# H stage: the low part of each slot product subtracted by GpSimd instead of VectorE, with the order of the stage hung on VectorE's last step

## The chip, the cores and the metric

The kernel runs on one core of a Trainium2 chip. The metric is the device time of one execution in microseconds (us), the median of a few runs. The engines of the core are TensorE (PE in the profile; its weight loads are PEld), VectorE (DVE), ScalarE (ACT), GpSimd (POOL) and SyncE (SP, which here issues the transfers).

## The reference

Block-causal attention over 8 batches and 8 heads (576 positions, head size 64), then a soft mixture of experts (32 slots, 8 experts), then a bilinear layer:

```python
x = attention(q, k, v)                  # 4608 x 512
logits = x @ phi                        # 4608 x 32
slot_input = softmax(logits, 0).T @ x   # 32 x 512
slot_out = experts(slot_input)          # 32 x 512, relu(si @ w1[e]) @ w2[e]
y = softmax(logits, 1) @ slot_out       # 4608 x 512, c @ slot_out
out = (((y @ w1) * (y @ w2)) @ w3) @ w_out
```

## The kernel before

The kernel uses that y has only rank 32. With A = slot_out @ w1 and B = slot_out @ w2 (32 x 1024 each), `(y @ w1) * (y @ w2)` is a sum over pairs of slots of c_s c_t A_s B_t. So it builds H, one row for each pair of slots, as the products of slots (A_s B_t + B_s A_t) times W = w3 @ w_out, and the last stage multiplies the products c_s c_t of each token by H.

The stages follow one another: attention with the gathering of the slots, then the experts mixed with the making of W, then the **H stage**, then the **final stage**. The change lies in the H stage.

The matmuls run on operands in the type fp32r, which is coarser than fp32. Every operand is therefore split in a high and a low part: ScalarE's copy makes the high part, a subtraction makes the low part, and three matmuls (high by high, high by low, low by high) make one product.

The H stage goes over eight blocks f of 128 columns of the hidden size. For each, `slot_products(f)` issues on VectorE two multiplications of 128x512 (L1114 into G, L1115 into T), their sum (L1116, in place in G), and a halving of 32 columns (L1119). ScalarE then casts G to the high part Gh (L1121), and VectorE subtracts G - Gh to make the low part Gl (L1122). `h_chunk(k, f)` issues three matmuls for each k from 0 to 3 (L1135), which sum over f in PSUM: 12 for one f, 96 in all. The pairs of a slot with its opposite are made by GpSimd in L1125 to L1127 and multiplied in `h_last` (L1141). L1160 to L1169 finish that part; L1169 is a VectorE subtraction that reads one operand from PSUM.

`evacuate(k)` takes a finished part of H out of PSUM: ScalarE's cast to Hhi (L1144) and VectorE's subtraction to Hlo (L1145).

The final stage goes over 12 groups of 384 tokens. `products(u)` makes the products of slot weights: VectorE multiplies four times (L1210) and once more for the half group (L1216), ScalarE casts (L1211, L1217, L1218), and the low parts are subtracted by VectorE for k = 0 and 2 and by GpSimd for k = 1 and 3 (L1213), and by VectorE in L1219. Then come the matmuls with H (L1238, L1240) and the copy out (L1241).

A scheduler orders the instructions of each engine, here as it sees fit, from a model of the times. Two things bind it. `tc.issue_after(ins)` puts VectorE's instructions of a block behind `ins` in VectorE's queue. Block f of the slot products stands behind L1119 of block f - 1. And `self.fences` collects one instruction for each f (entries 0 to 7) and one for each `evacuate` (entries 8 to 11); the final stage's first group stands behind entry 7, its second and third behind entry 11. `G_st` and `Gr_st` have four places, so block f writes where block f - 4 has been read.

Of the kernel before, what the change touches and what calls it, by code (L numbers as in the profile page):

```python
# [7 lines left out]
F32 = mybir.dt.float32  # L8
# [3 lines left out]
ALU = mybir.AluOpType  # L12
# [804 lines left out]
class Rest:  # L817
# [81 lines left out]
    def run(self, out):  # L899
        nc, tc, io, keep = self.nc, self.tc, self.io, self.keep  # L900
        ident = keep["ident"]
        with ExitStack() as ctx:
# [182 lines left out]
            for dc in range(4):  # L1085
                for g in range(4):
                    w = self.wA if g < 2 else self.wB
                    f = 512 * (g % 2)
# [19 lines left out]
            def slot_products(f):  # L1108

                G, T = G_st[f % 4][:, 0:512], G_st[f % 4][:, 512:1024]  # L1110
                rot = lambda t: bass.AP(t.tensor, t[:, f, 0:1].offset, [list(t.ap[0]), [4, 4], [1, 32], [1, 4]])
                flat = lambda t: bass.AP(t.tensor, t[:, f, 0:1].offset, [list(t.ap[0]), [0, 4], [1, 32], [0, 4]])
                cols = lambda t: t.rearrange("p (k s i) -> p k s i", k=4, i=4)
                nc.vector.tensor_tensor(cols(G), flat(AT), rot(BT), op=ALU.mult)  # L1114
                nc.vector.tensor_tensor(cols(T), flat(BT), rot(AT), op=ALU.mult)  # L1115
                nc.vector.tensor_tensor(G, G, T, op=ALU.add)  # L1116

                own = cols(G)[:, 0, :, 0]
                add = nc.vector.tensor_scalar(own, own, 0.5, None, op0=ALU.mult).ins  # L1119
                Gh, Gl = (Gr_st[f % 4][:, 512 * i:512 * i + 512] for i in range(2))  # L1120
                nc.scalar.copy(Gh, G)  # L1121
                return Gh, Gl, nc.vector.tensor_tensor(Gl, G, Gh.bitcast(F32), op=ALU.subtract).ins, add  # L1122


            nc.gpsimd.tensor_tensor(G16[:, :, 0:16], AT[:, :, 0:16], BT[:, :, 16:32], op=ALU.mult)  # L1125
# [5 lines left out]
            def h_chunk(k, f):  # L1131
                Gh, Gl = terms[f]
                Wh, Wl = w_terms[f]
                for i, (a, b) in enumerate(((Gh, Wh), (Gh, Wl), (Gl, Wh))):
                    nc.tensor.matmul(Hp[k], lhsT=a[:, 128 * k:128 * k + 128], rhs=b,  # L1135
                                     start=f == 0 and i == 0, stop=f == 7 and i == 2)


            def h_last(f):
                g = f % 4  # L1140
                nc.tensor.matmul(Hp[4][32 * g:32 * g + 32], lhsT=G16[:, f], rhs=W[f], start=f < 4, stop=f >= 4)  # L1141
# [4 lines left out]

            for f in range(8):
                with tc.issue_after(gfence) if f else nullcontext():
                    Gh, Gl, last_op, add = slot_products(f)
                gfence = add  # L1150
                terms[f] = Gh, Gl
                self.fences.append(last_op)
                if f < 6:
                    for k in range(4):
                        h_chunk(k, f)
                    h_last(f)
# [192 lines left out]
```

## Time and profile before

| | |
|---|---|
| median of 3 runs | 575.46 us (574.84 to 575.87) |
| profiled execution | 577.33 us |
| its span, first to last instruction | 575.5 us |
| mean granted clock of TensorE | 0.979 of full |
| H stage, from the first slot product to the last matmul of L1135 | 431.3 to 458.9 us |

The span is that of the profiled execution, in which 1.8 us lie around the instructions; times in the trace are us from the start of the span. Timeline rows merge neighbouring instructions of one line: "x2" is two, and the duration is that of both. Number in brackets is the time that the engine was idle before, and behind the arrow what ended it.

### The profile page before, as it was taken

Reading aid. Unit: us, or ns where it says so; the run is one execution under the profiler, and the core shown is the slowest. Engines: PE = TensorE matmul, PEld = TensorE weight load, DVE = VectorE, ACT = ScalarE, POOL = GpSimd, SP = SyncE. Lnnn points to the kernel's source line nnn. Section 1 sums busy time; section 2 is a strip of 40 time slices with the busy share of each in tenths; the row PEclk is TensorE's granted clock in tenths of the full one; section 3 lists DMA queues with packets and bytes.
Section 4 is the critical chain, followed back from the end, with each engine's and each line's share of the span. In section 5 each row is a group of like instructions: output and inputs, shape, how many; then the busy total and the mean of one; then the engine's idle time right before and its main releaser. Section 6 shows DMA issues by size and latency. Waiting matters only on the chain.

```text
span 575.5 us, 13898 instructions
## 1 busy us (share of the span) xinstructions
PE 554.7 (96%) x5470; PEld 418.6 (73%) x5470; DVE 397.6 (69%) x701; ACT 321.4 (56%) x625; POOL 336.5 (58%) x246
## 2 busy tenths in 40 slices
PE   6999999999999999999999869999999999999997
PEld 3887778787887787878878545565656778888885
DVE  6678798888988979889832548652619987647550
ACT  4656668586686686876855235423433453535441
POOL 6887897978979979889776019212532122313220
PEclk9899999999999999999999978999999989999999
DMA  7255666566547365665276647999904047564732
GB/s 250 90 179 187 208 251 225 160 204 210 169 168 225 119 225 161 205 208 170 80 237 216 267 165 303 409 421 426 412 10 151 14 135 234 175 230 161 234 122 109
DMA packets 39193, 116.96 MB, mean 203 GB/s; under 512 B 5324, under 2 KB 15548, under 8 KB 37064
## 3 DMA queue, kind: packets, MB, share of 16 engines
q1 hardware_dynamic: 38948, 116.00, 58.0%
q8 instruction: 43, 0.70, 0.5%
q14 instruction: 22, 0.18, 0.1%
q10 hardware_dynamic: 180, 0.07, 0.0%
HBM read 105.75 MB, written 10.45 MB: 202 GB/s over the span
## 4 chain that ended last, share of the span: by engine, by line
PE 87%; DVE 8%; DMA 2%; ACT 2%; issue 1%; ACTq 0%; DVEq 0%
PE ps L400 19%; PE ps L1238 18%; PE ps L433 15%; PE ps L938 6%; PE ps L360 5%; PE ps L449 4%; PE ps L557 3%; PE ps L1048 3%; PE ps L1020 3%; PE ps L500 2%; PE ps L606 2%; PE ps L1240 1%; DVE bm L364 1%; DMA win<-in_moe_w 1%; DVE g_stage L1116 1%; PE ps L45 1%
## 5 line engine op out<-in xcount | busy, mean ns | idle before, releaser
L364 DVE TENSOR_REDUCE bm<-ps 128x10 f32<-128x640 f32 (+2 forms) x128 | 122.2, 987 | 33.5 <-PE ps L360 23.8
L400 PE MATMUL ps<-set 64*128 64x320 f32 (+4 forms) x1152 | 112.7, 304 | 0.5 <-ACT PTb L408 0.4
L400 PEld LDWEIGHTS ps<-set 64*128 64x128 f32 x1152 | 89.8, 186 | 5.5 <-issue 1.6
L1238 PE MATMUL ps<-H,Ph 128*128 128x512 f32 x288 | 91.5, 400 | 1.7 <-DVE H L1145 1.7
L348 POOL TENSOR_TENSOR set<-raw,set 128x1152 fp32r<-128x1152 f32 x32 | 84.9, 2657 | 8.2 <-ACT set L341 7.0
L1213 POOL TENSOR_TENSOR Pl<-rot,Ph 128x384 fp32r<-128x384 f32 x24 | 29.9, 1263 | 90.7 <-ACT Ph L1211 90.7
L418 POOL TENSOR_TENSOR acc<-PTa,PTb 128x640 f32<-128x640 f32 x32 | 49.9, 1558 | 35.8 <-ACT PTb L408 26.5
L1238 PEld LDWEIGHTS ps<-H,Ph 128*128 128x128 f32 x288 | 55.0, 191 | 15.6 <-DVE H L1145 2.1
L400 PE MATMUL ps<-shift 64*128 64x320 f32 (+4 forms) x384 | 58.5, 299 | 0.0
L1238 PE MATMUL ps<-H,Pl 128*128 128x512 f32 x144 | 57.4, 399 | 0.0
L1241 ACT COPY o<-ps 128x512 f32<-128x512 f32 x36 | 21.1, 587 | 57.3 <-PE ps L1240 56.8
L938 PE MATMUL ps<-wo,w 128*128 128x512 f32 x192 | 51.5, 409 | 0.0
L418 POOL TENSOR_TENSOR acc<-acc,PTc 128x640 f32<-128x640 f32 x31 | 48.3, 1556 | 2.0
L408 ACT ACTIVATE PTa<-ps 128x1024 f32<-128x1024 f32 x32 | 32.9, 1027 | 27.9 <-PE ps L400 22.9
L360 PE MATMUL ps<-set 64*128 64x320 f32 (+4 forms) x384 | 46.5, 317 | 0.3 <-ACT set L344 0.2
L938 PEld LDWEIGHTS ps<-wo,w 128*128 128x128 f32 x192 | 34.3, 190 | 16.8 <-issue 9.6
L442 ACT COPY xT<-ps 128x320 f32<-128x320 f32 (+1 forms) x64 | 25.5, 399 | 36.7 <-PE ps L437 28.2
L408 ACT ACTIVATE PTc<-ps 128x640 f32<-128x640 f32 (+1 forms) x64 | 39.8, 651 | 8.1 <-PE ps L400 8.1
L433 PE MATMUL ps<-PTc,v 128*64 128x320 f32 (+1 forms) x256 | 43.6, 419 | 0.0
L491 POOL TENSOR_TENSOR xT<-xT,shift 128x576 f32<-128x576 f32 x28 | 39.5, 1423 | 0.0
L1210 DVE TENSOR_TENSOR rot<-rot,crep 128x384 f32<-128x384 f32 x48 | 34.7, 755 | 5.9 <-DMA rot<-cs 5.2
L341 ACT CAST set<-raw 128x1152 fp32r<-128x1152 f32 x31 | 35.6, 1150 | 3.6 <-DMA raw<-in_qk 3.6
(234 smaller groups left out, 1115.3 us busy)
## 6 DMA issues: line engine op xcount, KB each, us to landing
win<-in_moe_w SPq DMA_DIRECT2D x16, 2048.0 KB
raw<-in_qk SPq DMA_DIRECT2D x32, 576.0 KB
v<-in_v SPq DMA_DIRECT2D x32, 320.0 KB
rot<-cs SPq DMA_DIRECT2D x48, 192.0 KB
out<-o SPq DMA_DIRECT2D x11, 768.0 KB
raw<-in_moe_w SPq DMA_DIRECT2D x16, 512.0 KB
shift<-rr SPq DMA_DIRECT2D x56, 144.0 KB
w3raw<-in_w3T SPq DMA_DIRECT2D x14, 512.0 KB
```

Of the source, the lines that this page charges most:

```text
L341: self.nc.scalar.copy(hi, self.raw[n])
L348: self.nc.gpsimd.tensor_tensor(lo, self.raw.pop(n), hi.bitcast(F32), op=ALU.subtract)
L360: self.nc.tensor.matmul(ps[:, h, o:o + kn], lhsT=qh[r, q0:q0 + 128], rhs=kh[r, k0:k0 + kn], start=True, stop=True)
L364: self.nc.vector.tensor_reduce(self.bmb[n % 2][:, :, o:o + m // 64], self.st.pop(("M", n, i))[:, :, 0:m].rearrange("p h (n k) -> p h n k", ...
L400: self.nc.tensor.matmul(ps[:, h, o0:o0 + w], lhsT=lt[r, k] if i < 3 else lt[r], rhs=rt[r, q0:q0 + w], start=i == 0, stop=i == 3)
L408: self.nc.scalar.activation(out=out, in_=ps[:, :, 0:sum(g[3] for g in self.UNITS[u])], func=AF.Exp, scale=SCALE)
L418: eng.tensor_tensor(acc[:, :, lo:hi], a, b, op=ALU.add)
L433: mm(ps[64 * h:64 * h + 64, q0 - lo:q1 - lo], lhsT=v[:, 128 * j + 64 * h:128 * j + 64 * h + 64], rhs=pt[:, h, o:o + q1 - q0], start=j == 0 ...
L491: self.nc.gpsimd.tensor_tensor(x, x, self.rb[:, i], op=ALU.mult)
L938: nc.tensor.matmul(p, lhsT=a[:, o], rhs=b, start=c + i == 0, stop=c == 7 and i == 2)
L1210: nc.vector.tensor_tensor(p, p, crep, op=ALU.mult)
L1238: nc.tensor.matmul(ps, lhsT=a[:, k, r], rhs=b[:, k], start=n == 0, stop=False)
```

## The change

The subtraction that makes Gl is issued on GpSimd instead of VectorE. `slot_products` returns the halving L1119 (`add`), which as before is what the next block's VectorE instructions stand behind. It is now also what goes into `self.fences`: entry 7, behind which the final stage's first group stands on VectorE, was L1122 of block 7 and is now L1119 of block 7.

```diff
                 Gh, Gl = (Gr_st[f % 4][:, 512 * i:512 * i + 512] for i in range(2))
                 nc.scalar.copy(Gh, G)
-                return Gh, Gl, nc.vector.tensor_tensor(Gl, G, Gh.bitcast(F32), op=ALU.subtract).ins, add
+                nc.gpsimd.tensor_tensor(Gl, G, Gh.bitcast(F32), op=ALU.subtract)
+                return Gh, Gl, add
...
                 with tc.issue_after(gfence) if f else nullcontext():
-                    Gh, Gl, last_op, add = slot_products(f)
-                gfence = add
+                    Gh, Gl, gfence = slot_products(f)
                 terms[f] = Gh, Gl
-                self.fences.append(last_op)
+                self.fences.append(gfence)
```

## Rows read from the trace of the kernel before

**Rows 1.** The page: busy time by engine, and the chain that ended last.

```profile
PE 554.7 (96%) x5470; PEld 418.6 (73%) x5470; DVE 397.6 (69%) x701; ACT 321.4 (56%) x625; POOL 336.5 (58%) x246
...
PE 87%; DVE 8%; DMA 2%; ACT 2%; issue 1%; ACTq 0%; DVEq 0%
```

**Rows 2.** The chain in order of time (start, us, what), 425 to 475.

```profile
434.09 0.59 DVE g_stage L1114
434.68 0.60 DVE g_stage L1115
435.28 0.60 DVE g_stage L1122
435.89 1.71 DVE g_stage L1116
...
455.80 1.96 DVE rot L1210 x4
...
460.82 0.70 DVE H L1145
...
461.57 8.57 PE ps L1238 x29
```

**Rows 3.** The waits, 425 to 475: us in total, times, longest.

```profile
PE ps L1238 <- DVE H L1145: 1.7, 1, 1.7
...
DVE g_stage L1122 <- ACT g_stage L1121: 0.8, 1, 0.8
```

**Rows 4.** Busy time by stretch: PE, PEld, DVE, ACT, POOL, TensorE's granted clock, DMA.

```profile
458.90:462.30 3.40, 1.71 (x7) 1.13 (x7) 3.37 (x6) 2.82 (x6) 1.03 (x1) 1.00 0.24 64
462.30:465.70 3.40, 3.40 (x9) 2.66 (x9) 3.34 (x7) 1.19 (x3) 0.14 (x1) 0.50 0.83 253
465.70:469.10 3.40, 3.40 (x16) 2.74 (x16) 3.40 (x5) 1.75 (x4) 2.35 (x2) 1.00 0.18 59
```

**Rows 5.** The timeline of TensorE: the matmuls of blocks 4 to 7.

```profile
447.88 11.04 PE L1135 MATMUL ps<-W,g_stage 128*128 128x512 f32 x48
```

**Rows 6.** The timeline of VectorE: L1169, one turn, and the last block.

```profile
441.67 0.69 DVE L1169 TENSOR_TENSOR H<-ps,H 32x512 fp32r<-32x512 f32 x1
442.39 0.69 DVE L1122 TENSOR_TENSOR g_stage<-g_stage,g_stage 128x512 fp32r<-128x512 f32 x1
...
446.45 0.69 DVE L1114 TENSOR_TENSOR g_stage<-AB,AB 128x512 f32<-128x512 f32 x1
447.05 0.69 DVE L1115 TENSOR_TENSOR g_stage<-AB,AB 128x512 f32<-128x512 f32 x1
447.65 0.69 DVE L1122 TENSOR_TENSOR g_stage<-g_stage,g_stage 128x512 fp32r<-128x512 f32 x1
448.26 0.68 DVE L1116 TENSOR_TENSOR g_stage<-g_stage 128x512 f32<-128x512 f32 x1
448.97 0.20 DVE L1119 TENSOR_SCALAR g_stage<-g_stage 128x32 f32<-128x32 f32 x1
449.08 0.68 DVE L1114 TENSOR_TENSOR g_stage<-AB,AB 128x512 f32<-128x512 f32 x1
...
454.23 0.20 DVE L1119 TENSOR_SCALAR g_stage<-g_stage 128x32 f32<-128x32 f32 x1
455.19 0.69 DVE L1122 TENSOR_TENSOR g_stage<-g_stage,g_stage 128x512 fp32r<-128x512 f32 x1 [0.76 <-ACT g_stage L1121]
```

**Rows 7.** The timeline of GpSimd: subtractions without VectorE beside them, then with it.

```profile
423.28 2.52 POOL L1074 TENSOR_TENSOR g_stage<-wO,g_stage 128x512 fp32r<-128x512 f32 x2 [0.75 <-ACT g_stage L1073]
...
435.34 1.70 POOL L897 TENSOR_TENSOR W<-wO,W 128x512 fp32r<-128x512 f32 x1 [1.30 <-ACT W L896]
457.45 1.19 POOL L1213 TENSOR_TENSOR Pl<-rot,Ph 128x384 fp32r<-128x384 f32 x1 [20.41 <-ACT Ph L1211]
```

**Rows 8.** The timeline of VectorE in the same places.

```profile
435.20 0.68 DVE L1122 TENSOR_TENSOR g_stage<-g_stage,g_stage 128x512 fp32r<-128x512 f32 x1
435.81 1.78 DVE L1116 TENSOR_TENSOR g_stage<-g_stage 128x512 f32<-128x512 f32 x1
...
457.67 1.38 DVE L1216 TENSOR_TENSOR half<-half 32x384 f32<-32x384 f32 x1
```

**Rows 9.** The line L1216: ns min/median/max, first and last start.

```profile
L1216 DVE TENSOR_TENSOR half<-half x12: 539/546/1376, 457.7 to 544.7; 32x384 f32<-32x384 f32 x12
```

**Rows 10.** The timeline of all engines: VectorE with a PSUM operand beside GpSimd.

```profile
413.98 1.30 POOL L897 TENSOR_TENSOR w<-f,w 128x512 fp32r<-128x512 f32 x1 [0.73 <-ACT w L896]
414.01 0.69 DVE L842 SCALAR_TENSOR_TENSOR ps<-w3raw,ps 128x512 int32<-128x512 int32 x1
```

**Rows 11.** The timeline of ScalarE: the last cast of a slot product, the first evacuation.

```profile
454.54 0.62 ACT L1121 CAST g_stage<-g_stage 128x512 fp32r<-128x512 f32 x1 [2.01 <-DVE g_stage L1119]
...
458.27 0.59 ACT L1144 CAST H<-ps 128x512 fp32r<-128x512 f32 x1 [0.44 <-PE ps L1135]
```

## Prediction

> **What bounds the kernel now.** I read the page first: TensorE is busy for 96% of the span and carries 87% of the chain that ended last, VectorE 8% [rows 1]. A change to VectorE matters only where it is on that chain, so I read the chain in order of time next. From 434.09 to 461.5 us it is VectorE's queue without a break: the slot products of blocks 1 to 7, then the first group's products, then L1145 at 460.82, which releases the final stage's matmuls at 461.57 [rows 2]. From there TensorE carries it to the end. So the end of the kernel hangs on when VectorE reaches the first L1145, and a microsecond there is a microsecond of the total.
>
> The waits say the same from TensorE's side: one wait of 1.7 us for L1145 [rows 3]. [...]
>
> During the H stage itself TensorE isn't waiting: the 48 matmuls of blocks 4 to 7 take 11.04 us, 0.23 each and 2.72 for one block's twelve [rows 5]. VectorE's turn is 449.08 - 446.45 = 2.63 us a block [rows 6], so it stays just ahead. TensorE's queue isn't in the order of the source: in that order the first matmuls of block 7 would come at about 454.0 (447.88 + 27 x 0.227), but the cast that feeds them ends at 455.16 [rows 11] and the 48 have no gap. And the first evacuation starts only at 458.27 [rows 11], some nine matmuls into block 7, if block 7 starts at 447.88 + 36 x 0.227 = 456.04. So a block's eight matmuls on the high part go first and the four on the low part last. The low part has room of about 1.8 us; the high part has 456.04 - 455.16 = 0.9 us.
>
> **The change part by part.** All terms are changes of the start of the first L1145 in VectorE's queue, counted from L1119 of block 0, ahead of which the change puts nothing.
>
> Removed: the L1122 that stand between L1115 and L1116. Each takes 448.26 - 447.65 = 0.61 us of the queue [rows 6]; seven of them are 4.27 us. The last L1122 goes with its wait of 0.76 us for ScalarE: L1210 starts at 455.80 [rows 2], and could start 0.10 us after the start of L1119 at 454.23, as L1114 does behind L1119 (449.08 - 448.97 = 0.11) [rows 6]. That the fence is now L1119 allows it. This takes 455.80 - 454.33 = 1.47 us. Together -5.74 us.
>
> Added: eight subtractions of 128x512 on GpSimd. Alone such a one takes 2.52 / 2 = 1.26 us, up to 1.30 [rows 7, 10], twice VectorE's time; that by itself would hide in the 1.8 us of room and in GpSimd's idle time, since it did nothing between 437.04 and 457.45 [rows 7]. But it doesn't run beside VectorE. The one L897 that fell into the slot products, 435.34 to 437.04, took 1.70 us, and L1116 beside it 1.78 instead of 0.68 [rows 7, 8]. The ends tell how: VectorE's L1122 ended at 435.88, GpSimd at 437.04, 1.16 later, L1116 at 437.59, another 0.55 later. They took turns, each waiting for the other's whole work. The final stage repeats it with 384 columns: L1216, 0.55 us at the median, took 1.38 beside L1213 [rows 8, 9]. So each subtraction moved to GpSimd costs VectorE's queue 1.78 - 0.68 = 1.10 us, at a place where it is never idle. Eight are 8.80 us: seven among the slot products, and the eighth among the first group's products, which also stand before L1145. Bounds: the 384-column row gives 1.38 - 0.55 = 0.83 each, 6.64 in all; the time of a subtraction alone, 1.26 to 1.30, some 10.2. I take 1.10, since it is the row of this shape, in this stage, on the same line L1116 that will stand behind it.
>
> [...] If the hold were the full 1.28 us, the sum would be +3.8 us; the row shows 1.10, as part of the GpSimd instruction passes under VectorE's, and +2.3.
>
> Covered: VectorE's instruction with one operand in PSUM, L1169, takes 442.39 - 441.67 = 0.72 us of the queue now [rows 6]. Instructions of that kind ran beside GpSimd unstretched: L842 in 0.69 us under an L897 of 1.30 [rows 10]. In the queue L1169 stands between L1115 and the place of L1122, just where GpSimd's turn will come, so the work hides in one of the holds: -0.72 us. If the scheduler puts it elsewhere, that is 0.
>
> [...]
>
> Nothing else costs. GpSimd's queue has L897 of W's last block ahead of or behind the first Gl; it isn't needed until block 7, and its hold of VectorE is paid before and after alike. Behind the last Gl wait two L1213 of the first group, whose holds are also paid in both. ScalarE's casts and the transfers by SP stay as they are; SP's loads for later groups wait for L1210 and move with it.
>
> Sum: 8.80 - 5.74 - 0.72 = **+2.34 us** at the first L1145. The turn grows from 2.63 to 2.63 - 0.61 + 1.10 = 3.12 us, above TensorE's 2.72, so TensorE begins to wait 0.4 us a block once the 0.9 us of room is used up, about block 4. Its last block then starts 7 x 0.49 - 0.72 - 0.9 = 1.8 us later, and L1145, 2.3 later, is still what it waits for last. The clock's fall I leave as it is, once, behind a wait that is somewhat longer. Against the profiled execution's own 577.33 us this makes 579.67; the median of the runs is 1.87 us below it, so 575.46 + 2.34 = **577.8 us**.
>
> **The rivals.** First, faster: GpSimd fits into gaps and VectorE really loses its eight instructions. The price that decides is that of a hold: 8h = 6.46, so below h = 0.81 us the first L1145 comes earlier, and for 0.2% (1.15 us) it must be under 0.66. [...] For it: VectorE's queue would be 5.7 us shorter. Against it: the stretched rows [rows 8, 9].
>
> Second, the clock stays at 1.00. TensorE's idle time is spread over blocks 4 to 7 as waits of 0.4 us, and the long wait falls elsewhere. [...] Against it: the wait at the end isn't shorter than the one that now precedes the fall.
>
> Third, worse: TensorE's waits make the clock fall once more, or the scheduler, which believes the low parts come as GpSimd's time says, orders TensorE's or ScalarE's queue so that a late operand blocks more behind it. [...]
>
> **How the numbers follow.** The likeliest case has 0.62, with its own range from 576.9 (holds of 0.99 us) to 578.5 (L1169 not covered). The faster rival has 0.09, as both overlaps in the rows are stretched; the second 0.15, the third 0.14. About 0.2% (1.15 us) is what a measurement of this kernel can tell from no change. Holds as in the 384-column row, 6.64 - 5.74 - 0.72 = +0.18, would also be no change, 575.6 us; this I count with a little of the likeliest case, so the same has 0.18, slower 0.73, faster 0.09. The range, 575.6 to 579.6, runs from these short holds to the second fall of the clock, and takes in holds as long as a subtraction alone (10.2 - 6.46 = 3.7 us, 579.2).
>
> **What would show it.** GpSimd's new subtractions should last about 1.5 us (waiting for their turn), L1116 behind them 1.7 to 1.8, and VectorE's turn about 3.1 us. The last L1119 should come near 457, the first L1145 near 463.2, and TensorE should restart near 463.9. L1135 should show waits of 0.3 to 0.5 us from block 4 on for the casts. The prediction is wrong if L1116 stays at 0.68 us beside GpSimd, if the turn stays under 2.7 us, or if L1145 stops being what the final stage waits for.

## The result and the profile after

The changed kernel took 579.79 us (median of 6 runs, 578.45 to 580.83) against 576.14 us (6 runs, 574.84 to 576.83) for the kernel before: a ratio of 1.0066, with a 95% interval of 1.0048 to 1.0085. Run again later (e8 below), it took 579.31 us against 576.60, a ratio of 1.0043 (1.0028 to 1.0057) with 23 runs of the kernel before. By these medians the change makes the kernel slower by 2.7 to 3.7 us.

In the changed file the lines from L1123 on have moved by one: the matmuls of the H stage are L1136, the evacuations L1145 (ScalarE) and L1146 (VectorE), `h_last` is L1142 and GpSimd's products L1126 to L1128. From L1147 to the end the numbers are as before. L1122 is now GpSimd's subtraction.

The page of the kernel after, busy time by engine and the chain that ended last:

```profile
PE 555.8 (96%) x5470; PEld 417.5 (72%) x5470; DVE 400.0 (69%) x693; ACT 321.4 (56%) x625; POOL 348.3 (60%) x254
...
PE 85%; DVE 9%; ACT 3%; DMA 2%; issue 1%; ACTq 0%; DVEq 0%
```

Against [rows 1], eight instructions have left VectorE and yet it is busy for 2.4 us more. GpSimd has eight more and 11.8 us. An instruction that waits for its turn counts as busy, as the rows of L1116 below show (1.67 us instead of 0.68).

The chain of the kernel after in order of time (start, us, what):

```profile
434.79 0.59 DVE g_stage L1114
...
457.53 3.91 DVE rot L1210 x4
461.44 0.46 DVE half L1216
461.90 1.75 DVE Pl L1213 x2
...
463.68 0.55 DVE Ph L1219
...
464.26 0.70 DVE H L1146
...
465.01 8.36 PE ps L1238 x28
```

This answers to [rows 2]. It is still VectorE's queue that leads to TensorE's restart, at 465.01 instead of 461.57. The first halving, ahead of which nothing was changed, came 0.71 us later (434.46 against 433.75). Between the last products of the first group and the first evacuation there now stands L1219, which wasn't there.

The timeline of VectorE after: the block beside L897, L1169, and one turn.

```profile
437.71 1.17 DVE L1119 TENSOR_SCALAR g_stage<-g_stage 128x32 f32<-128x32 f32 x1
...
443.22 0.69 DVE L1169 TENSOR_TENSOR H<-ps,H 32x512 fp32r<-32x512 f32 x1
443.94 0.94 DVE L1116 TENSOR_TENSOR g_stage<-g_stage 128x512 f32<-128x512 f32 x1
...
451.27 0.68 DVE L1114 TENSOR_TENSOR g_stage<-AB,AB 128x512 f32<-128x512 f32 x1
451.88 0.68 DVE L1115 TENSOR_TENSOR g_stage<-AB,AB 128x512 f32<-128x512 f32 x1
452.60 1.67 DVE L1116 TENSOR_TENSOR g_stage<-g_stage 128x512 f32<-128x512 f32 x1
454.30 0.20 DVE L1119 TENSOR_SCALAR g_stage<-g_stage 128x32 f32<-128x32 f32 x1
454.40 0.69 DVE L1114 TENSOR_TENSOR g_stage<-AB,AB 128x512 f32<-128x512 f32 x1
```

And of GpSimd:

```profile
437.09 1.74 POOL L897 TENSOR_TENSOR W<-wO,W 128x512 fp32r<-128x512 f32 x1
...
452.18 1.54 POOL L1122 TENSOR_TENSOR g_stage<-g_stage,g_stage 128x512 fp32r<-128x512 f32 x1 [1.58 <-ACT g_stage L1121]
455.30 1.54 POOL L1122 TENSOR_TENSOR g_stage<-g_stage,g_stage 128x512 fp32r<-128x512 f32 x1 [1.59 <-ACT g_stage L1121]
458.43 1.30 POOL L1122 TENSOR_TENSOR g_stage<-g_stage,g_stage 128x512 fp32r<-128x512 f32 x1 [1.59 <-ACT g_stage L1121]
```

The turn is 454.40 - 451.27 = 3.13 us, where [rows 6] give 2.63. L1116 lasts 1.67 us: L1122 runs from 452.18 to 453.72, and L1116 ends at 454.27, 0.55 later, as in [rows 7, 8]. Beside L1169 the same L1116 needs only 0.94, since part of GpSimd's turn has passed under L1169.

TensorE after, the matmuls of blocks 4 to 7 (timeline), and what TensorE waited for (us in total, times, longest):

```profile
449.00 12.42 PE L1136 MATMUL ps<-W,g_stage 128*128 128x512 f32 x48 [0.17 <-ACT g_stage L1121]
```

```profile
PEld ps L1136 <- ACT g_stage L1121: 2.4, 5, 0.6
PE ps L1238 <- ACT H L1145: 2.2, 1, 2.2
...
PE ps L1238 <- DVE H L1146: 0.4, 1, 0.4
```

The 48 matmuls take 12.42 us instead of 11.04 [rows 5]; in the stage as a whole, weight loads waited five times for the casts; and the wait ahead of the final stage is 2.2 + 0.4 us instead of 1.7 [rows 3]. No wait of TensorE for GpSimd's L1122 shows in this stage.

Most of that last wait is for ScalarE. Three of its four evacuations stood ahead of L1217 and L1218 before (the first at 458.27 [rows 11]); now all four stand behind them, in ScalarE's timeline:

```profile
461.94 0.51 ACT L1217 CAST Ph<-half 32x384 fp32r<-32x384 f32 x1
462.47 0.51 ACT L1218 CAST Ph<-half 32x384 fp32r<-32x384 f32 x1
463.00 2.05 ACT L1145 CAST H<-ps 128x512 fp32r<-128x512 f32 x4
```

TensorE started on the final stage behind the first of these casts, at 463.64, and stopped once more for L1146. L1146 still ends the wait, but by little: without L1219 it would have started at about 463.68, when that cast had just ended.

Busy time by stretch after, in the columns of [rows 4]:

```profile
465.07:468.48 3.41, 3.41 (x8) 2.73 (x9) 3.41 (x7) 1.23 (x3) 0.18 (x1) 0.50 0.82 226
468.48:471.89 3.41, 3.41 (x16) 2.71 (x15) 3.41 (x5) 1.71 (x4) 2.31 (x2) 1.00 0.29 91
```

The granted clock falls once behind the wait, to 0.50 for 3.4 us as before, and 8 matmuls start in that stretch where the next holds 16. By the 9 and 16 of [rows 4] I estimate the price of such a stretch at 7/16 x 3.4 = 1.5 us.

### The profile page after: what moved, and what is told of

It reads as the page before. It is cut to its first block, busy times and chain, and to the rows that moved or that the text cites. A ratio compares the mean times of both kernels' runs of the same rounds, so it can differ in the third digit from the quotient of the medians.

```text
span 579.0 us, 13898 instructions
## 1 busy us (share of the span) xinstructions
PE 555.8 (96%) x5470; PEld 417.5 (72%) x5470; DVE 400.0 (69%) x693; ACT 321.4 (56%) x625; POOL 348.3 (60%) x254
## 4 chain that ended last, share of the span: by engine, by line
PE 85%; DVE 9%; ACT 3%; DMA 2%; issue 1%; ACTq 0%; DVEq 0%
PE ps L400 19%; PE ps L1238 18%; PE ps L433 15%; PE ps L938 6%; PE ps L360 5%; PE ps L449 4%; PE ps L557 3%; PE ps L1048 3%; DVE g_stage L1116 2%; PE ps L1020 2%; PE ps L500 2%; PE ps L606 2%; PE ps L1240 1%; DVE bm L364 1%; DMA win<-in_moe_w 1%
## 5 line engine op out<-in xcount | busy, mean ns | idle before, releaser
L400 PE MATMUL ps<-set 64*128 64x320 f32 (+4 forms) x1152 | 112.4, 303 | 0.5 <-ACT PTb L408 0.4
L1210 DVE TENSOR_TENSOR rot<-rot,crep 128x384 f32<-128x384 f32 x48 | 36.3, 797 | 5.7 <-DMA rot<-cs 5.3
```

The costliest lines, as they stand in the source:

```text
L400: self.nc.tensor.matmul(ps[:, h, o0:o0 + w], lhsT=lt[r, k] if i < 3 else lt[r], rhs=rt[r, q0:q0 + w], start=i == 0, stop=i == 3)
L1210: nc.vector.tensor_tensor(p, p, crep, op=ALU.mult)
```

## The experiments

Theory A is the prediction's: GpSimd's subtraction and a VectorE instruction with two operands in SBUF take turns, as L897 and L1116 did before (1.70 us, and 1.78 instead of 0.68 [rows 7, 8]), so each subtraction moved costs VectorE's queue about 1.1 us, at a place where the final stage waits for that queue. Theory B: what costs is that GpSimd is slow, so that the low parts reach TensorE late. Theory C: the new fence, and the order that the scheduler makes of it, carry the loss.

Three numbers from each profile tell where a kernel's time lies. The **head** is the start of block 0's halving (L1119; L1120 in e6, e7, e9 and e10), ahead of which the kernels don't differ, other than those with operands in PSUM (e6, e7, e9, e10). The **lead** is from there to the start of VectorE's first evacuation. The **tail** is from TensorE's restart behind that evacuation to the end of the span. For the kernel before: head 433.75, lead 460.82 - 433.75 = 27.07, tail 575.54 - 461.57 = 113.97. Its first halving, in VectorE's timeline:

```profile
433.75 0.33 DVE L1119 TENSOR_SCALAR g_stage<-g_stage 128x32 f32<-128x32 f32 x1
```

| kernel | head | lead | tail | ratio to before (95%) |
|---|---|---|---|---|
| before | 433.75 | 27.07 | 113.97 | |
| after | 434.46 | 29.80 | 114.03 | 1.0066 (1.0048 to 1.0085) |
| e1 fence alone | 434.20 | 26.79 | 112.48 | 0.9972 (0.9959 to 0.9985) |
| e2 extra subtractions | 434.74 | 34.98 | 115.13 | 1.0161 (1.0139 to 1.0184) |
| e3 extra fills | 434.86 | 27.13 | 114.01 | 1.0008 (0.9989 to 1.0028) |
| e4 half of them moved | 434.77 | 27.80 | 112.41 | 0.9988 (0.9976 to 0.9999) |
| e5 L1219 later | 432.69 | 29.21 | 112.41 | 1.0033 (1.0019 to 1.0047) |
| e6 B and T in PSUM | 436.19 | 24.55 | 112.36 | 0.9949 (0.9930 to 0.9967) |
| e7 the same, VectorE subtracts | 434.17 | 25.98 | 112.42 | 0.9971 (0.9955 to 0.9987) |
| e8 after, again | 433.65 | 29.79 | 113.98 | 1.0043 (1.0028 to 1.0057) |
| e9 A and T in PSUM | 434.36 | 24.67 | 112.57 | 0.9954 (0.9936 to 0.9972) |
| e10 the same, VectorE subtracts | 433.37 | 26.13 | 112.42 | 0.9980 (0.9963 to 0.9997) |
| e11 e5, profiled again | 433.07 | 29.22 | 114.01 | |
| e12 before, profiled again | 435.12 | 27.06 | 114.00 | |

The lead repeats within 0.02 us (before and e12, after and e8, e5 and e11). The head differs by up to 1.4 us between profiles of one kernel. The tail is near one of two values: 114.0, when the clock fell behind the wait, and 112.4 to 112.6, when it didn't. Only e2, where the clock stayed down twice as long, has 115.1.

**e1: the fence alone**, subtraction on VectorE.

```diff
-                self.fences.append(last_op)
+                self.fences.append(add)
```

> The subtraction stays on VectorE; only the fence entries are L1119 instead of L1122. Theory A (GpSimd's subtraction and VectorE's two-operand instructions take turns, some 1.1 us a piece): the turn stays at 2.63 us; VectorE's wait of 0.76 us before the last L1122 is filled, but L1219 now stands ahead of the first evacuation (0.58 us), so the first evacuation moves by about -0.2 us and the time by -0.2 +- 0.5 us. Theory C (the fence and the order that the scheduler makes of it carry the loss): +2 us or more.

Measured: lead 26.79, 0.28 us shorter, as theory A has it; all turns as before. The time fell by 0.28% (1.6 us; the medians, 575.65 and 576.86, are 1.2 us apart), more than expected. In its profile TensorE's wait ahead of the final stage was 0.9 us instead of 1.7, as another 0.5 now lay inside the H stage (from the first matmul's start in L1135 to the last one's 23.1 us, 22.6 before), and the clock didn't fall (tail 112.48). Theory C, that fence and order carry the loss, falls. VectorE's timeline at the end shows what the fence does to the order:

```profile
454.79 1.96 DVE L1210 TENSOR_TENSOR rot<-rot,crep 128x384 f32<-128x384 f32 x4
456.66 1.37 DVE L1216 TENSOR_TENSOR half<-half 32x384 f32<-32x384 f32 x1
457.96 0.67 DVE L1122 TENSOR_TENSOR g_stage<-g_stage,g_stage 128x512 fp32r<-128x512 f32 x1
458.56 1.82 DVE L1213 TENSOR_TENSOR Pl<-rot,Ph 128x384 fp32r<-128x384 f32 x2
460.42 0.55 DVE L1219 TENSOR_TENSOR Ph<-half,Ph 32x384 fp32r<-32x384 f32 x1
461.00 2.48 DVE L1145 TENSOR_TENSOR H<-ps,H 128x512 fp32r<-128x512 f32 x4
```

L1219 stands ahead of the evacuation here too: it is the fence, not GpSimd, that brings it there. ScalarE's evacuations stand behind L1217 and L1218 here as well.

**e2: eight more subtractions on GpSimd that nobody waits for**, in the kernel before.

```diff
+                nc.gpsimd.tensor_tensor(T, G, Gh.bitcast(F32), op=ALU.subtract)
                 return Gh, Gl, nc.vector.tensor_tensor(Gl, G, Gh.bitcast(F32), op=ALU.subtract).ins, add
```

> The kernel before, with eight more subtractions of the same form on GpSimd, whose results (written into T, which is done with) nobody reads. Theory A: eight holds of 1.1 us less 0.72 of L1169 that is hidden in one: VectorE's turn 3.7 us, L1116 at 1.7 us, the time +7 to +8 us. Theory B (what costs is that GpSimd's own slowness makes the low parts late for TensorE): 0, since nothing waits for the extra results.

Measured: lead 34.98, 7.9 us longer; turns of 3.73; the time 1.6% (9.3 us) longer, more than the 7 to 8 expected. In the timelines of VectorE (L1123 is the subtraction here) and of GpSimd the two meet at another instruction:

```profile
447.85 0.68 DVE L1115 TENSOR_TENSOR g_stage<-AB,AB 128x512 f32<-128x512 f32 x1
448.45 1.78 DVE L1123 TENSOR_TENSOR g_stage<-g_stage,g_stage 128x512 fp32r<-128x512 f32 x1
450.16 0.68 DVE L1116 TENSOR_TENSOR g_stage<-g_stage 128x512 f32<-128x512 f32 x1
```

```profile
448.08 1.61 POOL L1122 TENSOR_TENSOR g_stage<-g_stage,g_stage 128x512 f32<-128x512 f32 x1 [2.11 <-ACT g_stage L1121]
```

The tail is 1.1 us longer as well: ahead of the final stage TensorE waited 1.2 us for ScalarE's evacuation and then 2.2 us for VectorE's, and the clock was down for 6.8 us. Nothing waits for these results, and VectorE loses 1.78 - 0.68 = 1.10 us a piece. Theory B, that a slow engine's late results cost the time, falls: GpSimd's presence costs it.

**e3: eight fills on GpSimd**, in the kernel before.

```diff
+                nc.gpsimd.memset(T, 0.0)
                 return Gh, Gl, nc.vector.tensor_tensor(Gl, G, Gh.bitcast(F32), op=ALU.subtract).ins, add
```

> The kernel before, with eight fills of T (128x512) on GpSimd: it writes but reads nothing. [...] Theory B: 0.

Measured: lead 27.13, turns 2.63, ratio 1.0008: nothing. A fill of 0.58 us lay beside L1114 without stretching it, in the timelines of VectorE and of GpSimd:

```profile
447.51 0.20 DVE L1119 TENSOR_SCALAR g_stage<-g_stage 128x32 f32<-128x32 f32 x1
447.61 0.68 DVE L1114 TENSOR_TENSOR g_stage<-AB,AB 128x512 f32<-128x512 f32 x1
```

```profile
447.60 0.58 POOL L1122 MEMSET g_stage<- 128x512 f32 x1 [2.17 <-DVE g_stage L1116]
```

Only the halving beside a fill was stretched, in four of the eight blocks: from 0.20 to 0.60 us in three and from 0.33 to 0.80 in the first, and the turns stayed as they were within 0.06 us. Had fills of 0.52 to 0.58 us held VectorE for their length, eight would have cost about 4.4 us, an estimate from these lengths; the lead grew by 0.06. So the fills, which only write, didn't hold the two-operand instructions (0.68 us beside one); the subtraction, which reads, did (1.78 us in e2).

**e4: half of the subtractions moved**, in the changed kernel.

```diff
-                nc.gpsimd.tensor_tensor(Gl, G, Gh.bitcast(F32), op=ALU.subtract)
+                (nc.vector if f % 2 else nc.gpsimd).tensor_tensor(Gl, G, Gh.bitcast(F32), op=ALU.subtract)
```

> The changed kernel with the odd blocks' subtraction back on VectorE. Theory A: four holds (4.4 us) for four L1122 (2.4 us), less 0.72 (L1169 hidden) and 0.76 (the wait gone), plus 0.58 (L1219 ahead): +1.1 us against the kernel before, turns of 3.1 us behind even blocks and 2.6 behind odd ones. Theory B: half of the measured loss, +1.8 us, with all turns alike. Theory C: the full loss, +3.6 us.

Measured: lead 27.80, 0.73 us longer than before (1.1 expected). The turns alternate, 3.12 behind an even block and 2.63 behind an odd one, which only theory A has. The time didn't rise, though: 0.9988. The profile shows a wait of 0.9 us ahead of the final stage and a clock that stayed up, 1.6 us less tail. The expectation left that out. How often the clock stayed up in the other runs isn't known.

**e5: L1219 behind the first evacuation**, in the changed kernel.

```diff
-                nc.vector.tensor_tensor(Ph[32:64, 4], p, Ph[0:32, 4].bitcast(F32), op=ALU.subtract)
+                with tc.issue_after(self.fences[8]) if u == 0 else nullcontext():
+                    nc.vector.tensor_tensor(Ph[32:64, 4], p, Ph[0:32, 4].bitcast(F32), op=ALU.subtract)
```

> The changed kernel, with the first group's L1219 put behind the first evacuation on VectorE. If its place ahead of the evacuation is the term that the prediction left out, the first evacuation comes 0.58 us earlier after the last L1119 than in the changed kernel, and the time is about 0.5 us less than with the change; if TensorE has other things to wait for, 0.

Measured: lead 29.21, 0.59 us shorter than with the change. In the lead, then, the place of L1219 is worth what its row says. The time, 578.65 us against 579.31 for the changed kernel beside it (e8), fits with 0.66 less but doesn't show it, since the two intervals overlap.

**e6: the change, but with B and T in PSUM**, so that L1114 to L1116 (here L1115 to L1117) read one operand each from SBUF. B is also kept in SBUF, where GpSimd's products read it as before: four more copies on ScalarE.

```diff
+            Bp, Tp = keep["ps"][:, 2].rearrange("p (f s) -> p f s", f=8), keep["ps"][:, 0]
-            for m, dst in ((0, AT), (1, BT)):
+            for m, dst in ((0, AT), (1, Bp), (1, BT)):
...
-                G, T = G_st[f % 4][:, 0:512], G_st[f % 4][:, 512:1024]
+                G, T = G_st[f % 4][:, 0:512], Tp
...
-                nc.vector.tensor_tensor(cols(G), flat(AT), rot(BT), op=ALU.mult)
-                nc.vector.tensor_tensor(cols(T), flat(BT), rot(AT), op=ALU.mult)
+                nc.vector.tensor_tensor(cols(G), flat(AT), rot(Bp), op=ALU.mult)
+                nc.vector.tensor_tensor(cols(T), flat(Bp), rot(AT), op=ALU.mult)
```

> The changed kernel, with B also copied into PSUM and T kept in PSUM, so that L1114 to L1116 read only one operand each from SBUF. Theory A: VectorE and GpSimd run side by side: turn 2.0 to 2.1 us, no stretched L1116, GpSimd's subtraction 1.3 us; TensorE's matmuls then set the stage's pace at 2.72 us a block, and the wait of 1.7 us ahead of the final stage shrinks below 0.5 us: 572.5 to 574.5 us, faster than both kernels, less up to 0.8 us for the four more copies on ScalarE. Theory B: the low parts are as late as with the change, +3 us or more against the kernel before.

Measured: 573.79 us, ratio 0.9949, faster than both kernels, although the head holds a wait of 1.2 us of VectorE for the copy into PSUM. VectorE's and GpSimd's timelines:

```profile
448.99 0.69 DVE L1116 TENSOR_TENSOR ps<-ps,AB 128x512 f32<-128x512 f32 x1
449.71 0.69 DVE L1117 TENSOR_TENSOR g_stage<-g_stage,ps 128x512 f32<-128x512 f32 x1
```

```profile
449.29 1.30 POOL L1123 TENSOR_TENSOR g_stage<-g_stage,g_stage 128x512 fp32r<-128x512 f32 x1 [0.88 <-ACT g_stage L1122]
```

The same two instructions now lie over each other at the durations that they have alone, 0.69 and 1.30 us. The turn is 2.15 us, TensorE sets the stage's pace again, and its timeline shows no wait from the stage's 48 matmuls into the final stage:

```profile
449.95 11.04 PE L1137 MATMUL ps<-W,g_stage 128*128 128x512 f32 x48
460.83 1.16 PE L1239 MATMUL ps<-H,Ph 128*128 128x512 f32 x4
```

This is the direct test of theory A: with one operand of each of these three VectorE instructions out of SBUF, and the subtraction still on GpSimd, the loss turns into a gain of some 2.8 us. How much of it the operands in PSUM give by themselves is e7's question.

**e7: the same operands in PSUM, the subtraction on VectorE** (the edit of e6 in the kernel before).

> The kernel before (subtraction on VectorE) with the same operands in PSUM: what the PSUM copy does by itself. Theory A: only the one hold by L897 goes: the first evacuation 1.1 us earlier, turn still 2.63 us, the time -1.1 us, less up to 0.4 for the copies. Theory B: 0 to +0.5 us.

Measured: lead 25.98, 1.09 us shorter, turns of 2.62: the one hold by L897 is gone. The time is 0.29% (1.7 us) less, with the clock up in its profile. Of e6's gain, then, PSUM alone gives more than half (576.60 - 574.97 = 1.6 us), and moving the subtraction the rest (574.97 - 573.79 = 1.2 us).

**e8: the changed kernel once more.**

> The changed kernel itself once more. The two profiles put +2.73 us into the H stage and +0.71 us into what runs before it, where the instructions are the same. If that 0.71 us is chance, more runs give +2.7 +- 0.5 us; if it belongs to the change, +3.5 us or more, and the start of the slot products is again late by 0.7 us.

Measured: 579.31 us, 1.0043, medians 2.7 us apart; head 433.65, so not late this time; lead 29.79. The 0.71 us ahead of the stage was chance.

**e9: A instead of B in PSUM**, copied there by VectorE; ScalarE copies B, and A into SBUF for GpSimd.

```diff
-            for m, dst in ((0, AT), (1, BT)):
-                eng = nc.vector.tensor_copy if m == 0 else nc.scalar.copy
+            for m, dst in ((0, Ap), (1, BT), (0, AT)):
+                eng = nc.vector.tensor_copy if dst is Ap else nc.scalar.copy
```

> The changed kernel with A instead of B in PSUM (copied there by VectorE, which stands first; ScalarE then copies B and, for GpSimd alone, A into SBUF) and T in PSUM. Theory A: side by side as with B in PSUM, turn 2.15 us, TensorE never waits between the H stage and the final stage; the 1.2 us that VectorE waited for the copy of B into PSUM are gone, and TensorE's start in the stage no later than in the kernel before. That is the wait of 1.7 us and one stretch at half clock (1.5 us) less than the kernel before: -3.2 us, 0.5 to 1 us better than with B in PSUM. If the copies set the start after all, the same time as with B in PSUM, -2.8 us.

Measured: 574.17 us, 0.9954: faster than both kernels, but not better than e6, against the forecast. TensorE's start in the stage still waits for GpSimd's last product (1.1 us), which waits for both copies in SBUF. From VectorE's first copy to that start it takes 4.2 us here, 4.1 in e6 and 4.1 in the kernel before, so VectorE's wait of 1.2 us in e6 had not held TensorE up.

**e10: the same placement, the subtraction on VectorE** (the edit of e9 in the kernel before).

> The kernel before, subtraction on VectorE, with A and T in PSUM in the same way. It tells what the placement gives without moving the subtraction: turn 2.62 us, VectorE's queue again what the final stage waits for, first evacuation about 1.1 us earlier than in the kernel before: -1.1 us, or -1.6 to -2.6 us if the shorter wait keeps TensorE's clock up.

Measured: lead 26.13, 0.94 us shorter; 0.9980 (1.2 us less; the medians are 0.8 us apart). Beside e9, moving the subtraction gives another 1.4 us (575.61 - 574.17) with these operands in PSUM.

**e11, e12: two profiles once more.**

> The changed kernel with L1219 behind the first evacuation, profiled once more. In its first profile TensorE's clock did not fall behind the wait ahead of the final stage, and from the restart to the end it took 112.4 us, against 114.0 with the fall. If the fall belongs to the order of the work, it is absent again (112.4); if it varies from one execution to the next, it can be back (114.0). The first evacuation comes 28.9 us after the first L1119 either way.

> The kernel before, profiled once more: the same question. If the fall of the clock belongs to its wait of 1.7 us, it is there again and the end comes 114.0 us after the restart; if it varies, it can be absent (112.4). The first evacuation comes 26.7 us after the first L1119 either way.

Measured: e11 has lead 29.22 and tail 114.01: the fall of the clock, absent in e5, is back in the same kernel. e12 has lead 27.06, tail 114.00 and head 435.12, 1.37 us later than in the first profile of the same kernel. So the head varies from one execution to the next (before, e12), and so does the fall (e5, e11).

## Why the prediction was right or wrong

**The mechanism was right.** The stage lost what was forecast, by turn-taking: the turn is 3.12 to 3.13 us (3.12 forecast), TensorE's weight loads wait 0.5 to 0.6 us for the casts in each of blocks 4 to 7, and VectorE's first evacuation is what the final stage waits for last. e2, e3 and e6 (with e7 beside it) show the cause, each from another side. The change of the lead is 29.80 - 27.07 = +2.73 us against a forecast of +2.34, and 1.0043 in e8 against 577.8 / 575.46 = 1.0041. That it came this near is partly luck: within the stage the sum was 0.23 us too high, at its end 0.62 too low, as the next paragraphs show. One reading was loose: VectorE's queue isn't "without a break" in the chain before, which passes through ScalarE's cast L1121 at 454.54; the sum counts that wait (0.76 us) nevertheless.

**The hold of 1.10 us was right in sum, and made of two parts.** L1116 lasts 1.67 us, only 0.99 longer than alone. But it starts 452.60 - 451.88 = 0.72 us behind L1115, where [rows 6] have 0.60 from one instruction to the next. Before, L1122 stood between the two; now L1116 comes directly behind the L1115 whose T it reads, as L1119 comes behind the L1116 whose G it reads, 448.97 - 448.26 = 0.71 us later [rows 6]. No run isolates the cause.

**From the first halving to the last, +2.71 us forecast, +2.48 measured** (454.23 - 433.75 = 20.48 before, 457.42 - 434.46 = 22.96 after). L1169 was covered, as forecast; its turn was 3.47 us before and is 3.12 now, so it was worth 0.84 above the plain turn of 2.63, not 0.72. And L897's hold fell on the halving L1119, which took 1.17 us instead of 0.20, 0.97 where the one before cost 1.10. So the halving, which has a single input, in SBUF, was stretched beside GpSimd's subtraction too, which the prediction had not counted with.

**The step that failed in the sum** is the end of it: "That the fence is now L1119 allows it", with -1.47 us and then one hold of +1.10 before L1145, -0.37 us in all. It measured 6.84 - 6.59 = +0.25 us from the last halving to the first evacuation. The fence moved the first group forward as forecast (L1210 starts 0.11 us behind L1119), but with it came L1219, which the sum had put at nothing. The scheduler used to place it behind three evacuations, as VectorE's timeline of the kernel before shows:

```profile
460.82 1.89 DVE L1145 TENSOR_TENSOR H<-ps,H 128x512 fp32r<-128x512 f32 x3
462.74 0.55 DVE L1219 TENSOR_TENSOR Ph<-half,Ph 32x384 fp32r<-32x384 f32 x1
```

Now it places it ahead of all: 464.26 - 463.68 = 0.58 us. e1 shows that the fence brings it there, e5 that it is worth 0.59. Counting only the instructions that the fence had released in the old order missed it.

**The step that failed in the range** is the level: "so 575.46 + 2.34". The measured 579.79 lies 0.2 us above the range, whose shift was laid on three runs with a low median: the same kernel gave 576.14 (with three more runs), 576.86, 576.60 and 576.44 in the later sets. Laid on 576.14, the same range would have reached 580.3; with the 0.58 us of L1219 in the sum it would have reached 580.2. Either takes the measured time in, and e8's 579.31 lies inside the range as it stands, so on which side of it the time fell was also chance. The range had no term for what varies between executions: 1.4 us in the head and 1.6 in the fall of the clock. Its upper end takes in a second fall of the clock: no run of the change showed one (only e2 had the clock down for 6.8 us), and by the tails one fall costs 114.0 - 112.4 = 1.6 us.

**The rivals.** That GpSimd fits into gaps was wrong for this kernel, and right for e6, where neither side was stretched (0.69 and 1.30 us). That the clock stays up isn't a property of the change: it happened in e5 and not in e11. A second fall (the third rival) wasn't seen in the profiles of the change, but the reordering that this rival also names was: ScalarE's evacuations moved behind L1217 and L1218, and TensorE waited 2.2 us for the first of them.

**What stays open** is how often the clock falls in unprofiled runs, and so how much of the 1.6 us that e1 gained comes from it. Its lead accounts for only 0.28.

## What to carry to other kernels

Before work goes from VectorE to GpSimd, look in the trace for a place where the two already overlap: if an instruction there lasts longer than alone, the move can cost VectorE that stretch, here 1.10 us for every 0.61 saved. Keeping one operand of VectorE's instructions in PSUM took that stretch away here (0.69 us beside 1.30 in e6) and turned the same move into a gain of some 2.8 us. And when a fence is moved, look at everything behind it that can now come first, and put the forecast's range around the shift, not around one set of three runs.

## What the runs showed of the hardware

A GpSimd subtraction of 128x512 with both operands in SBUF and a VectorE instruction of that size with both in SBUF took turns: 1.26 to 1.30 us became 1.54 to 1.74, and 0.68 became 1.65 to 1.79. With one of VectorE's operands in PSUM both kept their own durations (0.69 and 1.28 to 1.30 us in e6). A fill by GpSimd stretched no two-operand instruction (e3). The halving, which has one operand, in SBUF, was stretched by both: from 0.20 to 1.17 us beside a subtraction, and to 0.60 beside a fill.

TensorE's granted clock fell to 0.50 for 3.4 us in six profiles: behind a wait of 1.7 us ahead of the final stage in before, e12 and e3, of 2.2 us in e11, and of 2.2 and 0.4 us in after and e8; in e2, with waits of 1.2 and 2.2 us, it was down for 6.8 us. It didn't fall, and the tail was 112.4 to 112.6 us, in e5, whose wait was 2.2 us like that of e11, the same kernel; with waits of 0.7 to 0.9 us in e1, e4, e7 and e10; and in e6 and e9, which had no such wait. A fall of 3.4 us cost 114.0 - 112.4 = 1.6 us.
